# 142 matrix products appended to the end of TensorE's list, in a convolution and two feed-forward layers

## Chip, cores and metric

The kernel runs on one core of one Trainium2 chip. The metric is the device time of one execution in microseconds, the median over runs.

## What is computed

An input of 2 x 4096 tokens with 192 channels goes through a causal convolution over 7 tokens, whose weights are a softmax per head (8 heads of 24 channels). Then come two feed-forward layers of 192 to 2048 to 192 channels. The reference, cut to what matters:

```python
def _attn_ref(x, weight):            # x (2, 4096, 192), weight (8, 7)
    w = softmax(weight, axis=-1)
    x_unf = x_pad[:, idx, :].reshape(B, S, K, H, group)
    return np.einsum('hk,bskhg->bshg', w, x_unf).reshape(B, S, D)

def _moe_ref(x, w_in, w_out):        # 8192 tokens, 192 -> 2048 -> 192
    h = x @ w_in
    return np.maximum(0.01 * h, h) @ w_out

def _moe2_ref(x, w_in, w_out):
    h = x @ w_in
    g = np.where(h >= 1, h, np.where(h <= -1, 0.0, (h + 1) ** 2 / 4))
    return g @ w_out
```

## The kernel before

Tokens are worked on in 16 tiles of 512 (T). Channels lie on partitions. Each feed-forward layer is cut into 16 slices of 128 inner channels, so there are 2 x 16 x 16 = 512 units of one layer, one tile and one slice. A unit has five products up (line 584, from x and the weights wi) and five down (line 593, from the activated values and the weights wo), since every value is held as a high and a low part in the type float32r. The weights of both layers stay on the chip in six tiles per kind: `wi_h`, `wi_l`, `wi_b`, `wo_h`, `wo_l`, `wo_b`, two of each, 128 partitions x 16 slices x 128 columns. They are written once, early in the run (lines 265 to 298).

The eight banks of the accumulator are tiles `banks[0]` to `banks[7]`. In the second part of the run units of both layers alternate; their up products go to banks 0 to 3 in turn, the sums of the first layer to banks 4 and 5, those of the second to banks 6 and 7.

Steps are put into a `Plan` with an engine, a cost and what they read and write. `plan.order()` lays them out in time with a list scheduler, and the loop in lines 776 and 777 calls each step's function in that order. The order in which instructions are made is the order of each engine's list; nothing reorders them later. Waits between engines are put in by the framework from what instructions read and write.

The last tile ends in `finish_last`: ScalarE copies bank 7 out (line 691), VectorE bank 6 (line 692), TensorE turns both by products with a folded identity (line 697, 64 columns each, float32) and by transposes (line 706) into banks 1 and 0, VectorE and ScalarE copy the turned blocks out (lines 714 and 723), and two DMAs store 192 KB each (line 732), one issued by SyncE and one by ScalarE. TensorE's list ends with the transposes of line 706.

At the start `add_warm` puts 24 products of a zero tile (bf16, 512 columns, line 328) on TensorE. Their sums are not read either.

Of the kernel before, what the change touches and what calls it, by code (L numbers as in the profile page):

```python
# [145 lines left out]
def kernel(  # L146
# [16 lines left out]
    nc = tc.nc  # L163
# [6 lines left out]
    T = 512  # L170
# [34 lines left out]
    banks = [pp.tile([128, T], F32, name=f"bank{i}") for i in range(8)]  # L205
# [22 lines left out]
    wi_h = [cp.tile([128, NF, 128], F32R, name=f"wi_h{m}") for m in range(2)]  # L228
    wi_l = [cp.tile([128, NF, 128], F32R, name=f"wi_l{m}") for m in range(2)]
    wi_b = [cp.tile([128, NF, 128], F32R, name=f"wi_b{m}") for m in range(2)]  # L230
    wo_h = [cp.tile([128, NF, 128], F32R, name=f"wo_h{m}") for m in range(2)]
    wo_l = [cp.tile([128, NF, 128], F32R, name=f"wo_l{m}") for m in range(2)]
# [88 lines left out]
    def add_warm():  # L321
        nc.gpsimd.memset(zero, 0.0)
        out_ = bank(1, -10)
        for i in range(WARM):
            cold = i < COLD
            plan.add(
                pe, 430 if cold else 220,
                lambda: nc.tensor.matmul(  # L328
                    out=out_(), lhsT=zero, rhs=zero.unsqueeze(1).broadcast_to((128, T // 128, 128)),
                    start=True, stop=True,  # L330
                ),
                writes=[out_], due=-1e9 if cold else 1e9,
            )
# [53 lines left out]
    def add_diagonals():  # L387
        def fold():
            for e in range(2):
                nc.gpsimd.tensor_copy(same[DB * e:DB * (e + 1)], ident[DB * e:DB * (e + 1), DB * e:DB * (e + 1)])  # L390

        plan.add(pool, 500, lambda: make_identity(nc, ident), writes=["ident"])
        plan.add(pool, 260, fold, reads=["ident"], writes=["same"])
        for k in range(KP, K):
            plan.add(
                dve, 220,
                lambda k=k: nc.vector.tensor_scalar(flat(NP + k - KP), ident, taps[:, 0, k:k + 1], None, ALU.mult),
                reads=["ident", "taps"], writes=[("diagonal a", k)], uses=[spare],
            )
        for k in range(NP):  # L400
            plan.add(
                dve, 220,
                lambda k=k: nc.vector.tensor_scalar(
                    flat(k).rearrange("p (e d) -> p e d", e=2), same.unsqueeze(1).broadcast_to((128, 2, DB)),
                    pair[:, k:k + 1], None, ALU.mult,
                ),
                reads=["same", "pair"], writes=[("diagonal", k)], uses=[spare],
            )
# [327 lines left out]
            )  # L736


    units = []
    for i in range(NF + OFF[-1]):  # L740
        for j in range(N0):
# [2 lines left out]
    one = [(0, j, f) for j in range(N0, NB) for f in range(NF)]  # L744
    two = [(1, j, f) for j in range(NB) for f in range(NF)]
    while two:
        units += one[:1] + two[:1]
        one, two = one[1:], two[1:]
# [12 lines left out]
    with tc.manual_schedule():  # L761
        add_warm()
        add_taps()
        add_diagonals()
        seen = set()
        for t, (m, j, f) in enumerate(units):
            if m == 0 and f == 0:
                add_conv(t - AHEAD, j)
            for o in range(2):
                if (m, o, f // 2) not in seen:  # L770
                    seen.add((m, o, f // 2))
                    add_weights(t, m, o, f // 2)
            add_unit(t, (m, j, f))
        for tag, count in COUNT.items():
            plan.rotate(tag, count)
        for n in plan.order():
            plan.steps[n]["fn"]()


# [28 lines left out]
```

## Time and profile before

| what | value |
|---|---|
| median of 2 runs | 1194.51 us (1194.39 to 1194.63) |
| span of the profiled execution | 1192.7 us |
| TensorE matmuls busy | 1186.8 us, 5210 instructions |
| TensorE weight loads busy | 972.7 us, 5210 instructions |
| VectorE / ScalarE / GpSimd busy | 782.7 / 734.3 / 438.2 us |
| bytes moved by DMA | 27.9 MB, 23 GB/s in the mean |

The span runs from the first to the last instruction of one profiled execution; the median is of runs without a profile. In the profile PE stands for TensorE's matmuls, PEld for its weight loads (each product has one of either; a float32 product has two), DVE for VectorE, ACT for ScalarE, POOL for GpSimd, SP for SyncE; a q behind an engine means its instruction queue. L593 is line 593 of the kernel. Matmuls are pipelined, so their recorded durations overlap; their pace is read from the distance of their starts. PEclk is the clock that TensorE was granted, as a share of full speed.

### The profile page before, as it was taken

The numbers are of one execution on the slowest core, as the hardware profiler recorded it, in microseconds if no ns is written. First come the engines' busy times: TensorE is split into PE (matmuls) and PEld (weight loads), VectorE is DVE, ScalarE is ACT, GpSimd is POOL, SyncE is SP. The second block draws the span as 40 slices with busy tenths as digits, with TensorE's granted clock in tenths as the row PEclk, the third lists the DMA queues.
The fourth block names the chain that finished last, engine by engine and source line by source line (L and its number), as shares of the span: only waits on it lengthen the run. The fifth ranks groups of instructions, "written<-read, shape, count | busy, mean of one in ns | idle before, by whom it ended". The sixth has DMA issues, their size and how long they took to land.

```text
span 1192.7 us, 15464 instructions
## 1 busy us (share of the span) xinstructions
PE 1186.8 (100%) x5210; PEld 972.7 (82%) x5210; DVE 782.7 (66%) x1209; ACT 734.3 (62%) x1296; POOL 438.2 (37%) x407
## 2 busy tenths in 40 slices
PE   9999999999999999999999999999999999999998
PEld 5788888888888888888888888888888888888887
DVE  7899897748567494764847658485674545447664
ACT  6777866656565565655656566565655656556654
POOL 4566374323223232232323233232233222335554
PEclk9999999999999999999999999999999999999999
DMA  4443111101001010010101001010000000000000
GB/s 132 117 104 99 43 43 18 23 1 23 10 9 23 1 23 9 15 18 1 32 1 23 10 10 23 1 23 1 1 14 1 14 1 3 12 1 14 14 14 14
DMA packets 114000, 27.90 MB, mean 23 GB/s; under 512 B 103680, under 2 KB 111872, under 8 KB 113920
## 3 DMA queue, kind: packets, MB, share of 16 engines
q1 hardware_dynamic: 113504, 26.69, 10.3%
q8 instruction: 40, 0.66, 0.2%
q14 instruction: 40, 0.33, 0.1%
q10 hardware_dynamic: 416, 0.23, 0.1%
HBM read 20.61 MB, written 6.29 MB: 23 GB/s over the span
## 4 chain that ended last, share of the span: by engine, by line
PE 99%; DMA 0%; SPq 0%; DVE 0%; issue 0%; ACT 0%; ACTq 0%
PE bank L584 49%; PE bank L593 49%; PE bank L529 1%; DMA wraw<-in_x_dram 0%; PE bank L534 0%; PE bank L328 0%; PE bank L478 0%; SPq L257 0%; PE bank L697 0%; SPq L255 0%; DVE s L714 0%; SPq L469 0%; DVE s L723 0%; ACT s L723 0%; ACTq L723 0%
## 5 line engine op out<-in xcount | busy, mean ns | idle before, releaser
L632 POOL TENSOR_TENSOR gl<-g,gh 128x512 fp32r<-128x512 f32 x256 | 343.2, 1343 | 677.6 <-ACT gh L630 674.7
L619 DVE TENSOR_SCALAR s<-bank 128x512 f32<-128x512 f32 x256 | 176.3, 689 | 303.4 <-PE bank L584 302.2
L584 PE MATMUL bank<-x,wi_h 128*128 128x512 f32 x1024 | 317.5, 391 | 0.0
L584 PE MATMUL bank<-x,wi_b 128*128 128x512 f32 x1024 | 316.9, 391 | 0.0
L623 ACT ACTIVATE s<-s,half 128x512 f32<-128x512 f32 x256 | 184.8, 722 | 192.7 <-DVE s L619 191.4
L630 ACT CAST gh<-g 128x512 fp32r<-128x512 f32 x256 | 158.6, 620 | 180.8 <-DVE g L627 178.1
L584 PEld LDWEIGHTS bank<-x,wi_h 128*128 128x128 f32 x1024 | 191.9, 188 | 42.2 <-issue 1.7
L584 PEld LDWEIGHTS bank<-x,wi_b 128*128 128x128 f32 x1024 | 192.2, 188 | 41.4 <-issue 1.4
L627 DVE TENSOR_TENSOR g<-bank,s 128x512 f32<-128x512 f32 x256 | 175.5, 686 | 67.8 <-ACT s L623 67.7
L593 PE MATMUL bank<-gh,wo_b 128*128 128x512 f32 x512 | 199.3, 389 | 0.0
L593 PE MATMUL bank<-gh,wo_h 128*128 128x512 f32 x512 | 199.3, 389 | 0.0
L593 PE MATMUL bank<-gl,wo_h 128*128 128x512 f32 x512 | 199.2, 389 | 0.0
L584 PE MATMUL bank<-x,wi_l 128*128 128x512 f32 x512 | 199.2, 389 | 0.0
L593 PE MATMUL bank<-gl,wo_b 128*128 128x512 f32 x512 | 199.2, 389 | 0.0
L593 PE MATMUL bank<-gh,wo_l 128*128 128x512 f32 x512 | 199.2, 389 | 0.0
L608 ACT ACTIVATE gh<-bank 128x512 fp32r<-128x512 f32 x256 | 152.8, 597 | 46.8 <-PE bank L593 25.3
L612 DVE TENSOR_TENSOR gl<-bank,gh 128x512 fp32r<-128x512 f32 x256 | 174.2, 680 | 9.8 <-ACT bank L608 9.2
L608 ACT ACTIVATE bank<-bank 128x512 f32<-128x512 f32 x256 | 151.8, 593 | 0.0
L523 DVE SCALAR_TENSOR_TENSOR xy<-xT,taps,xy 128x512 f32<-128x512 f32 x159 | 136.0, 878 | 0.2
L593 PEld LDWEIGHTS bank<-gl,wo_h 128*128 128x128 f32 x512 | 96.1, 188 | 20.0
L593 PEld LDWEIGHTS bank<-gh,wo_b 128*128 128x128 f32 x512 | 96.1, 188 | 20.0
L593 PEld LDWEIGHTS bank<-gh,wo_h 128*128 128x128 f32 x512 | 96.1, 188 | 20.0
(93 smaller groups left out, 741.5 us busy)
## 6 DMA issues: line engine op xcount, KB each, us to landing
xy<-in_x_dram SPq DMA_DIRECT2D x104, 64.0 KB, 2.4
wraw<-in_moe_w_out_dram SPq DMA_DIRECT2D x16, 384.0 KB, 3.0
out_dram<-o SPq DMA_DIRECT2D x90, 64.0 KB, 1.9
wraw<-in_moe_w_in_dram SPq DMA_DIRECT2D x16, 256.0 KB, 2.7
wraw<-in_moe_w_in_dram SPq DMA_DIRECT2D x32, 64.0 KB, 2.6
wraw<-in_x_dram SPq DMA_DIRECT2D x3, 384.0 KB, 5.3
out_dram<-s SPq DMA_DIRECT2D x1, 192.0 KB, 2.0
out_dram<-s ACTq DMA_DIRECT2D x1, 192.0 KB, 2.0
```

The costliest lines, as they stand in the source:

```text
L523: nc.vector.scalar_tensor_tensor(out=ys[i](), in0=t()[:, i, k:k + T], scalar=taps[:, i, k:k + 1], in1=ys[i](), op0=ALU.mult, op1=ALU.add,)
L529: nc.tensor.matmul(out=ys[1](), lhsT=flat(k), rhs=t()[:, 1, 2 * k:2 * k + T], start=(k == 0), stop=(k == NP - 1))
L584: nc.tensor.matmul(out=h(), lhsT=w, rhs=v[:, k], start=(part == 0 and i == 0), stop=(part == 1 and i == 1))
L593: nc.tensor.matmul(out=p[part](), lhsT=w, rhs=v(), start=(first and i == 0), stop=(last and i == len(todo) - 1))
L608: lambda dst=dst: nc.scalar.activation(out=dst(), in_=h(), func=ACTF.Prelu, alpha=0.01),
L612: dve, 680, lambda: nc.vector.tensor_tensor(out=b(), in0=h(), in1=a(), op=ALU.subtract),
L619: dve, 680, lambda: nc.vector.tensor_scalar(s(), h(), 1.0, -1.0, ALU.min, ALU.max),
L623: act, 720, lambda: nc.scalar.activation(out=s(), in_=s(), func=ACTF.Square, scale=0.5, bias=half),
L627: dve, 680, lambda: nc.vector.tensor_tensor(out=g(), in0=h(), in1=s(), op=ALU.max),
L630: plan.add(act, 620, lambda: nc.scalar.copy(a(), g()), reads=[g], writes=[a])
L632: pool, 1390, lambda: nc.gpsimd.tensor_tensor(out=b(), in0=g(), in1=a(), op=ALU.subtract),
```

## The change

A function `add_more` is added and called once, after the loop that makes all steps. It makes 142 products on TensorE, each with `start` and `stop`, into banks 2 to 7. Weights come from `wo_h` and `wo_l` of both layers, the moving values from `wi_h` and `wi_l`. `low` and `high` are partitions 0 to 63 and 64 to 127: a product with these uses half the rows of the array. In order: 6 plain products (128 rows, 512 columns); 24 pairs of a low half (bank 2) and a high half (bank 3); 4 plain; 24 pairs into banks 6 and 7, where the high half uses other weights than the low one; 4 plain; 12 short ones (64 columns); 8 times a plain and a short one; 4 plain. No instruction reads what they leave in the banks.

```diff
--- before.py
+++ after.py
@@ -736,6 +736,41 @@
             )
 
 
+    def add_more():
+
+        def flat_(t):
+            return t.rearrange("p f c -> p (f c)")
+
+        streams = [flat_(wi_h[0]), flat_(wi_l[0]), flat_(wi_h[1]), flat_(wi_l[1])]
+        weights = [flat_(wo_h[0]), flat_(wo_l[0]), flat_(wo_h[1]), flat_(wo_l[1])]
+        full, low, high = slice(0, 128), slice(0, 64), slice(64, 128)
+
+        def one(k, at, rows=full, cols=T):
+            w = weights[k % 4][rows, 128 * (k % 16):128 * (k % 16 + 1)]
+            v = streams[k // 4 % 4][rows, T * (k % 4):T * (k % 4) + cols]
+            nc.tensor.matmul(out=banks[at][:, 0:cols], lhsT=w, rhs=v, start=True, stop=True)
+
+        for k in range(6):
+            one(k, 2 + k % 2)
+        for k in range(24):
+            one(k, 2, low)
+            one(k, 3, high)
+        for k in range(4):
+            one(k, 4 + k % 2)
+        for k in range(24):
+            one(k, 6, low)
+            one(k + 7, 7, high)
+        for k in range(4):
+            one(k, 4 + k % 2)
+        for k in range(12):
+            one(k, 4, cols=64)
+        for k in range(8):
+            one(k, 5)
+            one(k + 3, 4, cols=64)
+        for k in range(4):
+            one(k, 4 + k % 2)
+
+
     units = []
     for i in range(NF + OFF[-1]):
         for j in range(N0):
@@ -775,6 +810,7 @@
             plan.rotate(tag, count)
         for n in plan.order():
             plan.steps[n]["fn"]()
+        add_more()
 
 
 # ---- launch: one core; inputs and outputs as the reference has them ----
```

## Rows read from the trace of the kernel before

**Rows 1.** The page, part 1: span; busy time, share and instructions by engine.

```profile
span 1192.7 us, 15464 instructions
PE 1186.8 (100%) x5210; PEld 972.7 (82%) x5210; DVE 782.7 (66%) x1209; ACT 734.3 (62%) x1296; POOL 438.2 (37%) x407
```

**Rows 2.** The page, part 4: the chain that ended last, shares by engine.

```profile
PE 99%; DMA 0%; SPq 0%; DVE 0%; issue 0%; ACT 0%; ACTq 0%
```

**Rows 3.** Windows: length, busy time (instructions) by engine, PEclk, DMA share, GB/s.

```profile
100.00:1180.00 1080.00, 1080.00 (x4765) 893.70 (x4764) 693.13 (x1048) 655.48 (x1125) 378.27 (x315) 1.00 0.08 15
```

**Rows 4.** Timeline near the end: start, length, engine, line, operation.

```profile
1185.38 0.39 PE L593 MATMUL bank<-gh,wo_h 128*128 128x512 f32 x1
1185.38 0.19 PEld L593 LDWEIGHTS bank<-gh,wo_l 128*128 128x128 f32 x1
1185.60 0.39 PE L593 MATMUL bank<-gh,wo_l 128*128 128x512 f32 x1
1185.61 0.19 PEld L593 LDWEIGHTS bank<-gl,wo_h 128*128 128x128 f32 x1
```

**Rows 5.** Chain in order of time, its last run of products: start, length, what.

```profile
1181.69 5.68 PE bank L593 x25
```

**Rows 6.** Timeline from 1186.9 us to the end, some lines left out.

```profile
1186.98 0.39 PE L593 MATMUL bank<-gl,wo_h 128*128 128x512 f32 x1
1187.36 0.97 PEld L697 LDWEIGHTS bank<-same,yz 128*128 128x128 f32 x8 [0.41 <-ACT yz L691]
1187.36 1.10 PE L697 MATMUL bank<-same,yz 128*128 128x64 f32 x8
1187.41 0.69 DVE L692 COPY xy<-bank 128x512 f32<-128x512 f32 x1 [3.38 <-PE bank L593]
1188.19 0.48 PEld L706 LDWEIGHTS bank<-ident,xy 128*128 128x128 f32 x4
1188.30 0.61 PE L706 MATMUL bank<-ident,xy 128*128 128x128 f32 x4
...
1189.40 0.39 SPq L732 DMA_DIRECT2D out_dram<-s  x1
1189.46 0.37 ACT L723 COPY s<-bank 128x256 f32<-128x256 f32 x1 [2.15 <-DVE s L723]
1189.86 0.40 ACTq L732 DMA_DIRECT2D out_dram<-s  x1
```

**Rows 7.** By line, 732 and 803: landing time of the stores; closing instructions, first and last start.

```profile
DMA to landing us min/median/max: 2.0/2.0/2.0
...
L803 SPq EVENT_SEMAPHORE  x7: 17/28/28, 1189.8 to 1192.6; - x7
```

**Rows 8.** By line, 298, 426 and 627: durations (ns), first and last start.

```profile
L298 POOL TENSOR_TENSOR wo_l<-wa,wo_h x16: 730/738/1200, 24.6 to 188.3; 128x256 fp32r<-128x256 f32 x16
...
L426 DVE TENSOR_TENSOR x<-bank,x x21: 676/680/692, 17.0 to 1089.4; 128x512 fp32r<-128x512 f32 x21
...
L627 DVE TENSOR_TENSOR g<-bank,s x256: 644/692/693, 136.8 to 1183.3; 128x512 f32<-128x512 f32 x128
```

**Rows 9.** Groups by line, 1187.3 to 1189: busy us, mean ns of one, idle before.

```profile
L697 PE MATMUL bank<-same,yz 128*128 128x64 f32 x8 | 1.1, 281 | 0.0
L697 PEld LDWEIGHTS bank<-same,yz 128*128 128x128 f32 x8 | 1.0, 191 | 0.4 <-ACT yz L691 0.4
```

**Rows 10.** Line 328's products: two runs of the timeline, then all 24 by line.

```profile
1.07 4.87 PE L328 MATMUL bank<-zero 128*128 128x512 bf16 x11 [1.07 <-POOL own L340]
...
18.10 1.47 PE L328 MATMUL bank<-zero 128*128 128x512 bf16 x6
...
L328 PE MATMUL bank<-zero x24: 377/390/634, 1.1 to 19.2; 128*128 128x512 bf16 x24
```

**Rows 11.** Windows at the end, columns as in Rows 3.

```profile
1190.00:1191.00 1.00, 0.00 (x0) 0.00 (x0) 0.00 (x0) 0.00 (x0) 0.00 (x0) 1.00 0.72 242
1191.00:1192.00 1.00, 0.00 (x0) 0.00 (x0) 0.00 (x0) 0.00 (x0) 0.00 (x0) 0.55 0.45 151
```

## The prediction

> **What bounds the kernel now.** I read the page's busy times first: the span is 1192.7 us and TensorE's matmuls are busy for all but 6 us of it [rows 1]. The chain that ended last is TensorE for 99% [rows 2]. The middle of the run, by windows, holds 4765 products in 1080 us at a granted clock of 1.00 [rows 3], one every 0.227 us; the timeline shows such products starting 0.22 to 0.23 us apart, each recorded as 0.39 us long (they overlap), and the load of the next weights beginning as the product before starts [rows 4]. The chain in order of time says the same for the last run of them: 25 in 5.68 us, 0.227 each [rows 5].
>
> So what stands on TensorE's list is paid in full, unless something else lasts longer. That is so only at the very end: the last four transposes end at 1188.30 + 0.61 = 1188.91, while the second store is issued at 1189.86 [rows 6], lands 2.0 us later, at about 1191.9, and is followed by some 0.8 us of closing semaphores [rows 7]. So TensorE is idle for the last 3.8 us of the span.
>
> The profiled execution's span is 1192.7 and the median of the runs 1194.5, so 1.8 us lie around the span; I add the difference of the spans to the median.
>
> **The change part by part.** Nothing is removed or moved, no DMA, no copy. 142 products are added behind the last transpose: 26 plain ones (128 rows, 512 columns: 6 + 4 + 4 + 8 + 4), 96 half-row ones (64 rows, 512 columns, two rows of 48) and 20 short ones (128 rows, 64 columns: 12 + 8).
>
> What they wait for: the weights were written by 188.3 us; banks 4 and 5 were last read by 1090.1 us; the last read of an h bank that I look for in banks 2 and 3 began at 1183.3 [rows 8]; banks 6 and 7 are copied out by 1187.41 + 0.69 = 1188.10 [rows 6]. All of it lies before 1188.91, so no wait is added, and nobody waits for the products. The stores run as before. The transposes' weight loads follow each other at (0.97 - 0.191) / 7 = 0.111 us, by the eight loads just ahead of them [rows 6, 9]. The last transpose starts 0.27 us before its end, at 1188.64, so the first new product starts at about 1188.75.
>
> Plain products: 26 x 0.227 = 5.90 us [rows 5].
>
> Short products: the nearest rows are the eight with 64 columns near the end, (1.10 - 0.281) / 7 = 0.117 us apart [rows 6, 9], hardly more than a load: weights, not columns, bound them. Those are another fp32 form. From below nothing goes under the load's 0.111, from above stands the 512-column 0.227: 2.2 to 4.5 us for twenty. I take 0.117: 2.34 us.
>
> Half-row products: the trace has none, every product in it uses 128 rows. Two bounds for a pair. If the halves run one after the other, a pair costs two products: 2 x 0.227 = 0.454. If they run side by side, it costs one product, 0.227, and not less than its two loads, 2 x 0.111 = 0.222. Which is nearer? The halves share neither array rows, nor the partitions that they read, nor the bank that they write (2 and 3, then 6 and 7), and a load already runs under a product [rows 4]. I take side by side, at 0.235, a little above 0.227 because loads and columns are nearly equal limits there: 48 x 0.235 = 11.28 us.
>
> On the loads the rows are plain: the next whole-row load starts at 1185.38 and 1185.61, with the product in flight [rows 4]. The Trainium skill, "TensorE: Matmul & The Clock Gate", Part 3, The mechanism, says under "What overlaps and what doesn't" that a load overlaps products in flight only where their row groups differ. This trace does not agree for whole rows; by that sentence a half's load would stand behind the same half's product, 0.338 a pair, and the sum would give 1216.6 (the second rival). The same part, Measured speedup, gives 3.07 times for four 32-row tiles, which I turn into an estimate of 4 / 3.07 = 1.30 product times for a group, 0.295 a pair and 1214.6 in all; no row here shows it.
>
> Changing between whole rows and half rows happens four times. From below it is free; from above a product's tail (0.39 - 0.227 = 0.16) plus a load that is not covered (0.19 [rows 4]) make 0.35. I take the tail alone: 4 x 0.16 = 0.64 us.
>
> Sum: 5.90 + 2.34 + 11.28 + 0.64 = 20.16, and the last product's tail of 0.16. TensorE ends at 1188.75 + 20.16 + 0.16 = 1209.07. The closing after the store took about 0.8 us; some of it may have been waits that are over by then, so 0.3 to 0.8; with 0.8 the span is 1209.9, 17.2 us longer. The first 3.1 us of the products lie beside the store and cost nothing; were that cover gone, the change would cost 20.3. Time: 1194.5 + 17.2 = 1211.7 us, 1.4% more. Its own range, by a pair of 0.222 to 0.295 and the small bounds, is 1209 to 1215.
>
> **The rivals.**
>
> *The halves one after the other (the other side).* Place: the two rows of 24 pairs. For it: TensorE issues in order, and none of the 512-column products in these rows starts less than 0.216 us after another [rows 3, 5, 10]. Against it: no products there had different rows. Price: 48 x (0.454 - 0.235) = 10.5 us more, 1222.2, 2.3% over. The 2% line lies at 23.9 us more than before, 6.7 above my sum: this mechanism decides from a pair of 0.235 + 6.7 / 48 = 0.375 us on.
>
> *Side by side, but loads not covered.* A half's weights could be held back until the product in the same half is through: 0.111 + 0.227 = 0.338 a pair, 48 x 0.103 = 4.9 us more, 1216.6. For it: whether the spare set of weights that [rows 4] imply exists for each half apart is not seen. Against it: the whole-row loads.
>
> *The clock falls.* After TensorE went quiet at 1188.91 the granted clock went from 1.00 to 0.50 between 1191 and 1192 [rows 11], so the row of 1187.36 to 1188.91 with its thin products did not at once bring it down. What slow products cost shows at the start: 11 warm-up products with 512 columns at (4.87 - 0.63) / 10 = 0.42 us, later six at (1.47 - 0.39) / 5 = 0.22 [rows 10]. If half-row products passed for little work and the clock stayed at its lower level (1.2 GHz) through them, pairs would double: 48 x 0.235 = 11.3 more, 1223.0, and 1227.5 with the 20 plain ones behind the first row at twice 0.227. Against it: side by side they are as dense as plain ones. If it fell only behind the short ones, 12 plain products would double, 2.7 us, 1214.4, inside my range.
>
> *The products do not run.* Their sums are not read. But the 24 warm-up products, whose sums nobody reads either, are all in the trace [rows 10]. Time then 1194.5.
>
> **How the numbers follow.** Side by side 0.63 (1211.7); loads not covered 0.12 (1216.6); one after the other 0.17 (1222.2); clock down 0.06 (1223 to 1227); not run 0.01; a gain from something that I do not see 0.01. I predict the likeliest, 1211.7. The range 1209 to 1223 takes in the first three and leaves out about 0.13: the clock, the rest, and the ends of the bounds. Faster and slower are counted from 2%, about what a measurement of this kernel can tell from no change. Same: 0.63 + 0.12 + 0.01 = 0.76; slower: 0.17 + 0.06 = 0.23; faster 0.01.
>
> **What would show it.** In the profile of the changed kernel: the first new product starts at 1188.7 to 1188.9 with no idle before it but the load's; each half row lasts 24 x 0.235 = 5.6 us, and low and high products start in twos about 0.11 apart, 0.235 from low to low. A half row of 8.1 us would mean uncovered loads, 10.9 us one after the other, with starts 0.227 apart and a clock of 1.00; a clock of 0.50 there the third rival. The short ones stand 0.11 to 0.12 apart, the span ends at most 0.8 us behind TensorE, and everything before 1188.6 stays where it was. I am wrong if the pair takes 0.30 us or more.

## The result, and the profile after

The changed kernel takes 1211.47 us in the median (1211.44 to 1211.50), against 1194.51 before: a ratio of 1.014, 95% interval 1.011 to 1.017. The forecast was 1211.7. The span grew from 1192.7 to 1209.7 us, by 17.0 (forecast: 17.2).

The page of the changed kernel, the span and the busy times (the lines that answer to [rows 1]):

```profile
span 1209.7 us, 15748 instructions
...
PE 1206.7 (100%) x5352; PEld 989.0 (82%) x5352; DVE 782.5 (65%) x1209; ACT 734.4 (61%) x1296; POOL 438.1 (36%) x407
```

PE and PEld have 142 instructions more each, the counts of the others are unchanged. The products all run. The chain in order of time for the last 23 us shows that they now end the program (start, length, what):

```profile
1186.85 0.47 PE bank L593 x2
1187.31 1.09 PE bank L697 x8
1188.40 0.45 PE bank L706 x4
1188.85 19.99 PE bank L751 x141
```

Line 751 is the one product call of the added function. Up to 1188.85 the chain holds the same steps as before [rows 6]. Behind them stand 19.99 us of new products; the last ends at 1188.85 + 19.99 = 1208.84, and the span ends 0.86 us later. (The chain counts 141 of the products; the page has all 142.)

The timeline of TensorE in the changed kernel (start, length, engine, line, operation, count) shows the first row of pairs with the change into it and out of it, a piece of the second row, and the short ones:

```profile
1189.62 0.39 PE L751 MATMUL bank<-wi_l,wo_h 128*128 128x512 f32 x1
1189.84 0.40 PE L751 MATMUL bank<-wi_l,wo_l 128*128 128x512 f32 x1
1190.16 0.50 PE L751 MATMUL bank<-wi_h,wo_h 64*128 64x512 f32 x2
1190.50 0.40 PE L751 MATMUL bank<-wi_h,wo_l 64*128 64x512 f32 x2
1190.74 0.39 PE L751 MATMUL bank<-wi_h,wo_h 64*128 64x512 f32 x2
1190.97 0.40 PE L751 MATMUL bank<-wi_h,wo_l 64*128 64x512 f32 x2
...
1195.51 0.39 PE L751 MATMUL bank<-wi_l,wo_l 64*128 64x512 f32 x2
1195.83 0.50 PE L751 MATMUL bank<-wi_h,wo_h 128*128 128x512 f32 x1
...
1196.96 0.49 PE L751 MATMUL bank<-wi_h,wo_h 64*128 64x512 f32 x1
1196.96 0.50 PE L751 MATMUL bank<-wi_l,wo_l 64*128 64x512 f32 x1
...
1203.81 0.28 PE L751 MATMUL bank<-wi_h,wo_h 128*128 128x64 f32 x1
1203.92 0.28 PE L751 MATMUL bank<-wi_h,wo_l 128*128 128x64 f32 x1
```

Here a line with 64x512 and x2 is a pair. Its length, 0.39 us, is that of one product: both halves are recorded as starting and ending together. From 1190.74 to 1195.51 a pair follows every 0.227 us. At a change from whole to half rows, the step is 0.32 (1189.84 to 1190.16) and the next one 0.34 (to 1190.50) where 0.227 would stand without it. The short ones stand 0.11 us apart. In the second row, where the high half has other weights, the first pair starts together as well.

The windows of the changed kernel over the two rows and the short ones (columns as in [rows 3]):

```profile
1190.10:1195.50 5.40, 5.40 (x47) 4.42 (x48) 0.00 (x0) 0.00 (x0) 0.00 (x0) 1.00 0.22 73
1196.90:1202.30 5.40, 5.40 (x47) 4.62 (x48) 0.00 (x0) 0.00 (x0) 0.00 (x0) 1.00 0.00 0
1203.60:1207.60 4.00, 4.00 (x29) 3.65 (x28) 0.00 (x0) 0.00 (x0) 0.00 (x0) 1.00 0.00 0
```

From its first pair to the plain product behind it the first row of 48 half products takes 5.67 us (1190.16 to 1195.83), the change out of it included; 48 products one after the other would take 10.9. The granted clock is 1.00 in all three windows.

### The profile page after: what moved, and what is told of

Same layout as the page of the kernel before. It is cut to its first block, busy times and chain, and to the rows that moved or that the text cites. A ratio compares the mean times of both kernels' runs of the same rounds, so it can differ in the third digit from the quotient of the medians.

```text
span 1209.7 us, 15748 instructions
## 1 busy us (share of the span) xinstructions
PE 1206.7 (100%) x5352; PEld 989.0 (82%) x5352; DVE 782.5 (65%) x1209; ACT 734.4 (61%) x1296; POOL 438.1 (36%) x407
## 4 chain that ended last, share of the span: by engine, by line
PE 99%; DMA 0%; SPq 0%; issue 0%
PE bank L584 48%; PE bank L593 48%; PE bank L751 2%; PE bank L529 1%; DMA wraw<-in_x_dram 0%; PE bank L534 0%; PE bank L328 0%; PE bank L478 0%; SPq L257 0%; PE bank L697 0%; SPq L255 0%; PE bank L706 0%; SPq L469 0%
## 5 line engine op out<-in xcount | busy, mean ns | idle before, releaser
L584 PEld LDWEIGHTS bank<-x,wi_l 128*128 128x128 f32 x512 | 96.1, 188 | 20.0
L593 PEld LDWEIGHTS bank<-gl,wo_b 128*128 128x128 f32 x512 | 96.1, 188 | 20.0
L593 PEld LDWEIGHTS bank<-gh,wo_l 128*128 128x128 f32 x512 | 96.1, 188 | 20.0
```

Source lines behind the costliest of these rows:

```text
L584: nc.tensor.matmul(out=h(), lhsT=w, rhs=v[:, k], start=(part == 0 and i == 0), stop=(part == 1 and i == 1))
L593: nc.tensor.matmul(out=p[part](), lhsT=w, rhs=v(), start=(first and i == 0), stop=(last and i == len(todo) - 1))
```

## The experiments

Theory: the halves run side by side because they use different rows of the array, so that a pair costs one product. Rivals: another bank alone is what lets them; the engine looks far ahead in its list; loads limit a pair; changes between whole and half rows cost nothing or more; thin work brings the clock down. Each experiment changes only the added products.

**Both products in the low half** (`same_half`):

```diff
-            one(k, 3, high)
+            one(k, 3, low)
...
-            one(k + 7, 7, high)
+            one(k + 7, 7, low)
```

> Both products of every pair now use the low half (partitions 0 to 63); banks, counts and order stay. If different array rows are what lets two products run side by side, each half product costs 0.227 us and a pair 0.454 instead of 0.227: 48 x 0.227 = 10.9 us more than the changed kernel's 1211.5, so 1222.4. If different banks are enough, the time stays at 1211.5. If a half's load must stand behind the product in the same half (the rival with uncovered loads), each half product costs 0.338: 48 x 0.449 = 21.6 us more, 1233. If half-work lets the granted clock fall, it shows as 0.50 in the windows of the two rows and about 1240 or more.

Measured: 1222.39 us, 1.023 of before (1.021 to 1.025). Chain, and timeline of products and of loads:

```profile
1188.88 30.85 PE bank L751 x142
```

```profile
1190.77 0.62 PE L751 MATMUL bank<-wi_h,wo_l 64*128 64x512 f32 x2
1191.23 0.62 PE L751 MATMUL bank<-wi_h,wo_h 64*128 64x512 f32 x2
...
1190.54 0.42 PEld L751 LDWEIGHTS bank<-wi_h,wo_l 64*128 64x128 f32 x2
1191.00 0.42 PEld L751 LDWEIGHTS bank<-wi_h,wo_h 64*128 64x128 f32 x2
```

A pair now lasts 0.62 and follows every 0.46 us: one after the other. The rows are the same 64, the banks still differ, so another bank is not enough. Nor does a half-row product simply cost half: it costs the 0.227 of a whole one. (Both products now also read the same partitions; a product's rows and its partitions go together, so no run tells the two apart.) A pair's two loads also come one product apart (0.42 for two of 0.19) and lie under products in flight in the same half: half products of one half keep the 0.227 pace, and the rival with uncovered loads, 1233, is out. So is the rival of the clock, as it was put: two rows of half products, 10.9 us each, did not lower it. Windows (columns as before):

```profile
1195.00:1200.00 5.00, 5.00 (x24) 4.06 (x23) 0.00 (x0) 0.00 (x0) 0.00 (x0) 1.00 0.00 0
1205.00:1210.00 5.00, 5.00 (x23) 4.06 (x23) 0.00 (x0) 0.00 (x0) 0.00 (x0) 1.00 0.00 0
```

The clock column alone would not settle it: in the kernel before it reads 1.00 at 2 to 3 us as well, where the warm-up products took 0.42 us each [rows 10]:

```profile
2.00:3.00 1.00, 1.00 (x4) 0.35 (x3) 0.00 (x0) 0.77 (x2) 0.80 (x6) 1.00 0.06 14
```

The pace settles it. 122 products of 512 columns at 0.227, 20 short ones at 0.112, four changes at 0.21 and the last product's tail of 0.16 come to 30.9 us, and the chain has 30.85: there is no room for a slow stretch.

The Trainium skill's sentence that a load overlaps products in flight only where the row groups differ ("TensorE: Matmul & The Clock Gate", Part 3, The mechanism) does not describe these rows either: same half, load under product.

**Whole rows** (`whole_rows`), the half products made of 128 rows:

```diff
-            one(k, 2, low)
-            one(k, 3, high)
+            one(k, 2)
+            one(k, 3)
...
-            one(k, 6, low)
-            one(k + 7, 7, high)
+            one(k, 6)
+            one(k + 7, 7)
```

> All half products become whole-row products of 128 rows; counts, banks and order stay. Pace 0.227 each: 48 x 0.227 = 10.9 us more, and the four changes between whole and half rows go away. If a change costs 0.2 us as the changed kernel's starts suggest, that gives 1222.4 - 0.8 = 1221.6; if changes cost nothing, 1222.4.

Measured: 1221.57 us (ratio 1.022, 1.021 to 1.024). The chain:

```profile
1188.85 29.99 PE bank L751 x142
```

That is 29.99 against 30.85 us in the experiment ahead of it: 142 products at the same pace, without the four changes. 0.86 / 4 = 0.21 us for a change.

**All low halves, then all high ones** (`low_then_high`):

```diff
             one(k, 2, low)
+        for k in range(24):
             one(k, 3, high)
...
             one(k, 6, low)
+        for k in range(24):
             one(k + 7, 7, high)
```

> The same 142 products, but in each row the 24 low halves stand first and the 24 high ones behind them. If products start in the order of the list and only neighbours overlap, each row takes 48 x 0.227 = 10.9 us instead of 5.5, the time is 1211.5 + 10.9 = 1222.4 less one overlap a row. If the engine looks ahead far enough to bring a high product beside a low one, the time stays near 1211.5.

Measured: 1220.89 us (ratio 1.022, 1.020 to 1.023). The order in the list matters: most of the gain is gone (9.4 of 10.9 us), so the engine doesn't look far ahead. But it looks further than I expected: one overlap a row would have given 1222.4 - 2 x 0.227 = 1221.9, and 1.0 us less was measured. Timeline around the seam of the first row:

```profile
1194.76 0.39 PE L751 MATMUL bank<-wi_l,wo_h 64*128 64x512 f32 x1
1194.77 0.49 PE L751 MATMUL bank<-wi_h,wo_h 64*128 64x512 f32 x1
1194.99 0.39 PE L751 MATMUL bank<-wi_l,wo_l 64*128 64x512 f32 x1
1195.10 0.39 PE L751 MATMUL bank<-wi_h,wo_l 64*128 64x512 f32 x1
1195.21 0.39 PE L751 MATMUL bank<-wi_l,wo_h 64*128 64x512 f32 x1
1195.33 0.39 PE L751 MATMUL bank<-wi_h,wo_h 64*128 64x512 f32 x1
1195.44 0.39 PE L751 MATMUL bank<-wi_l,wo_l 64*128 64x512 f32 x1
```

The four lines with wi_l are the last four low products, the three with wi_h the first high ones. The first high product is recorded as starting at 1194.77, beside the twenty-first low one and ahead of three that stand before it in the list. The time agrees: about 0.75 us saved in each row is some three products.

**Pairs of 64 columns** (`thin_pairs`):

```diff
-            one(k, 2, low)
-            one(k, 3, high)
+            one(k, 2, low, 64)
+            one(k, 3, high, 64)
...
-            one(k, 6, low)
-            one(k + 7, 7, high)
+            one(k, 6, low, 64)
+            one(k + 7, 7, high, 64)
```

> The 48 pairs get 64 columns instead of 512, so that loads bound them. My prediction counted two loads one after the other, 0.222 a pair: 48 x 0.222 = 10.7 us, 1211.3, hardly a change. If the loads of the two halves run at once, as the equal starts in the first row of the changed kernel suggest, a pair costs 0.111: 48 x (0.227 - 0.111) = 5.6 us less, 1205.9. If such thin work lets the granted clock fall, windows show 0.50 behind them and the 12 to 20 us around are slower by up to twice.

Measured: 1205.70 us (ratio 1.011, 1.008 to 1.014). Timeline, products and loads:

```profile
1190.34 0.28 PE L751 MATMUL bank<-wi_h,wo_h 64*128 64x64 f32 x2
1190.45 0.28 PE L751 MATMUL bank<-wi_h,wo_l 64*128 64x64 f32 x2
1190.56 0.28 PE L751 MATMUL bank<-wi_l,wo_h 64*128 64x64 f32 x2
...
1190.31 0.19 PEld L751 LDWEIGHTS bank<-wi_h,wo_h 64*128 64x128 f32 x2
1190.42 0.19 PEld L751 LDWEIGHTS bank<-wi_h,wo_l 64*128 64x128 f32 x2
```

There is a pair every 0.111 us, with two loads in the length of one. The loads of the two halves run at once. My floor of two loads, 0.222, does not exist. One of the four runs took 1213.65 at a mean granted clock of 0.993, the others 1205.6 to 1205.7 at 1.000. That run has no trace, so where its clock fell is not known; the last experiment shows such a fall in full.

**Quarter rows** (`quarters`), 192 products of 32 rows in place of 96 of 64:

```diff
-            one(k, 2, low)
-            one(k, 3, high)
+            for q in range(4):
+                one(k, 2 + q, slice(32 * q, 32 * q + 32))
...
-            one(k, 6, low)
-            one(k + 7, 7, high)
+            for q in range(4):
+                one(k + 7 * q, 2 + q, slice(32 * q, 32 * q + 32))
```

> Each pair of 64-row halves becomes four products of 32 rows (array rows 0, 32, 64, 96) with banks 2 to 5, 192 in place of 96. If four row groups run side by side as two do, a group of four costs 0.227 and the time stays at 1211.5. The Trainium skill's 3.07 times for four tiles (TensorE: Matmul & The Clock Gate, Part 3, Measured speedup), as an estimate 1.30 product times a group. In rows of this case: at 0.295 a group the time would be 48 x 0.068 = 3.3 us more, 1214.8; if only two at a time run, 0.454 a group and 1222.4.

Measured: 1211.50 us (ratio 1.014, 1.012 to 1.016), the changed kernel's own time.

```profile
1190.72 0.40 PE L751 MATMUL bank<-wi_h,wo_h 32*128 32x512 f32 x4
1190.73 0.19 PEld L751 LDWEIGHTS bank<-wi_h,wo_l 32*128 32x128 f32 x4
1190.95 0.40 PE L751 MATMUL bank<-wi_h,wo_l 32*128 32x512 f32 x4
```

In this timeline four products and four loads run at once, a group every 0.23 us. The estimate from the Trainium skill's 3.07 times ("TensorE: Matmul & The Clock Gate", Part 3, Measured speedup), 1.30 product times a group, is not what this case shows: 1.00.

**Many changes** (`many_turns`), the same 142 products, twelve plain ones each behind four pairs:

```diff
-        for k in range(6):
-            one(k, 2 + k % 2)
...
+        for k in range(2):
+            one(k, 4 + k % 2)
+        for k in range(48):
+            if k < 24:
+                one(k, 2, low)
+                one(k, 3, high)
+            else:
+                one(k - 24, 6, low)
+                one(k - 17, 7, high)
+            if k % 4 == 3:
+                one(k // 4, 4 + k // 4 % 2)
```

> The same 142 products, but 12 of the plain ones now stand one behind every fourth pair, so that the list changes between whole and half rows 24 times instead of 4. My prediction took 0.16 us a change (bounds 0 to 0.35); the starts in the changed kernel suggest 0.2: 20 x 0.2 = 4 us more, 1215.5. If a change costs nothing, 1211.5; at 0.16, 1214.7; at 0.35, 1218.5.

Measured: 1215.73 us (ratio 1.018, 1.016 to 1.019), 4.26 more than the changed kernel for 20 more changes: 0.213 us each. Timeline around two of them, with loads:

```profile
1189.89 0.19 PEld L751 LDWEIGHTS bank<-wi_h,wo_l 64*128 64x128 f32 x2
1190.12 0.40 PE L751 MATMUL bank<-wi_h,wo_l 64*128 64x512 f32 x2
1190.45 0.19 PEld L751 LDWEIGHTS bank<-wi_h,wo_h 128*128 128x128 f32 x1 [0.36 <-issue]
1190.45 0.50 PE L751 MATMUL bank<-wi_h,wo_h 128*128 128x512 f32 x1
1190.88 0.19 PEld L751 LDWEIGHTS bank<-wi_l,wo_h 64*128 64x128 f32 x2 [0.24 <-issue]
```

The load for the plain product doesn't start with the pair in flight, as it does elsewhere, but 0.33 us after that pair's start: across a change it starts late. From the pair at 1190.12 to the pair at 1190.88 the step is 0.76 us, where two steps of 0.227 make 0.45. The two changes there cost 0.31 between the starts; the rest of 2 x 0.213 comes behind them, like the step of 0.34 behind 1190.16 in the changed kernel.

**Ten plain products only** (`ten_plain`):

```diff
-        for k in range(6):
+        for k in range(10):
             one(k, 2 + k % 2)
-        for k in range(24):
...
-            one(k, 4 + k % 2)
```

> Only ten plain products of the 142 are left. By the prediction they start at 1188.7, end by 1191.2 and lie beside the last store, which lands at about 1191.9: the time is that of before, 1194.5, and the span 1192.7. If work behind the last transpose is not covered by the store, it is 10 x 0.227 = 2.3 us more, 1196.8.

Measured: 1194.38 us, ratio 0.9997 (0.9988 to 1.0006), span 1192.7. Timeline:

```profile
1189.82 0.40 ACTq L732 DMA_DIRECT2D out_dram<-s  x1
...
1190.79 0.40 PE L751 MATMUL bank<-wi_h,wo_l 128*128 128x512 f32 x1
```

The tenth product ends at 1191.19, before the store issued at 1189.82 has landed 2.0 us later. These 2.3 us of work on TensorE cost nothing.

**142 short products** (`all_short`):

```diff
-        for k in range(6):
-            one(k, 2 + k % 2)
...
+        for k in range(142):
+            one(k, 2 + k % 2, cols=64)
```

> All 142 added products are whole-row products with 64 columns. Bound by loads at 0.111 to 0.117 each they take 15.8 to 16.6 us, TensorE ends at about 1205 and the time is 1207.3 to 1208. If the granted clock falls under such thin work, a window of the second half shows 0.50; if loads slow down with it, the time rises by up to 8 us, to 1215.

Measured: 1217.09 us (1216.39 to 1217.94; ratio 1.019, 1.017 to 1.020), above both sums. Windows and timeline:

```profile
1190.00:1192.00 2.00, 2.00 (x20) 2.00 (x19) 0.00 (x0) 0.00 (x0) 0.00 (x0) 1.00 0.59 197
1192.00:1194.00 2.00, 2.00 (x16) 2.00 (x15) 0.00 (x0) 0.00 (x0) 0.00 (x0) 0.77 0.00 0
1194.00:1196.00 2.00, 2.00 (x12) 2.00 (x11) 0.00 (x0) 0.00 (x0) 0.00 (x0) 0.50 0.00 0
```

```profile
1192.71 0.28 PE L751 MATMUL bank<-wi_l,wo_h 128*128 128x64 f32 x1
1192.82 0.28 PE L751 MATMUL bank<-wi_l,wo_l 128*128 128x64 f32 x1
...
1194.28 0.40 PE L751 MATMUL bank<-wi_l,wo_l 128*128 128x64 f32 x1
1194.49 0.40 PE L751 MATMUL bank<-wi_l,wo_h 128*128 128x64 f32 x1
```

At about 1193.1 the granted clock goes from 1.00 to 0.50, its lower level of 1.2 GHz, though PE and PEld are recorded as busy without a break; it stays there to the end. The pace goes from 0.111 to 0.213 us, loads included. My upper bound of 1215 was too low because the fall came after 4.4 us and some 40 products, so that 102, more than the half I had reckoned with, ran at the slow pace: 40 x 0.111 + 102 x 0.213 = 26.2 us, which is the 26.23 of its chain. The profiled run took 1217.77; two others took 1216.4. If only the point of the fall differs, it came some 14 products later there (an estimate: 1.4 / 0.102), so the 40 are no fixed count.

## Why the prediction was right, point by point

*What bounds the kernel.* Right. Work at the end of TensorE's list was free where it ended ahead of the store's landing (`ten_plain`), and of the change's 19.99 us all but 3.0 were paid (17.0 in the span).

*Start and closing.* The first new product is recorded at 1188.60 (forecast 1188.75, at the earliest 1188.7), but the second follows 0.32 us later instead of 0.227, and the chain has the new products take over at 1188.85. TensorE ends at 1208.84 (forecast 1209.07), and the span 0.86 us later (0.8). The 188.3 us by which the weights were to be written is the start of their last write, which took at most 1.2 us [rows 8]; nothing hangs on it.

*The halves.* Right, and shown by three runs: side by side in different array rows (changed kernel), one after the other in the same rows with different banks (`same_half`), one after the other, but for some three a row, when they are not neighbours in the list (`low_then_high`). The pair costs 0.227, not 0.235: 48 x 0.008 = 0.4 us too much. The reason I gave for the surcharge, loads as a nearly equal limit, is wrong (`thin_pairs`). With it went the one visible sign that I had wrong: I expected low and high products 0.11 us apart, and they start together.

*The changes between whole and half rows.* Taken at 0.16 each, measured at 0.21 in two ways (`whole_rows` against `same_half`, and `many_turns`): 4 x 0.05 = 0.2 us too little. The term held the tail of a product alone, but the load comes late as well (`many_turns`); how the 0.21 divides between the two is not shown. The upper bound of 0.35 held.

*The short ones.* The twelve in a row stand 0.112 us apart against 0.117: 20 x 0.005 = 0.1 too much. That loads bound them fits `thin_pairs`.

These misses, -0.4, +0.2 and -0.1, add up to -0.3 us: the new products took 19.99 us in the chain against 20.16 + 0.16 = 20.32. They took over 0.1 us later than forecast, so TensorE ended 0.2 earlier. That the total came so close owes something to the different signs, which is luck.

*The range.* 1209 to 1215 is not what its bounds add up to. With all of them at once the sum goes from 1209.8 (pairs 0.222, shorts 0.111, changes free, closing 0.3) to 1217.5 (0.295, 0.227, 0.35). The measured time lies in both.

*The rivals.* One after the other: its price was right to 0.2 us (1222.2, and `same_half` 1222.39), its condition not met. What spoke for it, that TensorE issues in order, does not hold strictly either: in `low_then_high` a product started ahead of three others. Loads not covered: not met, in either half arrangement. The clock: right as a mechanism, on the wrong products. Half rows keep it at 1.00; a long run of 64-column products brought it down (`all_short`). Its price is now read at both levels: 0.111 us at 1.00, 0.213 at 0.50. Through the 12 short ones and the 8 mixed in with plain ones in the change it stayed at 1.00. That products may be dropped: not so, all 142 are in the trace.

## What to carry to other kernels

Products with 64 or 32 rows can be had side by side for the price of one (here 0.227 us with 512 columns), if neighbours in the list use different rows of the array; the same products sorted by half lose most of it. In every run the products of a pair or group also had different banks; whether one bank would do was not tried. Keep products of one row size together, since each change between whole and half rows cost 0.21 us. And when work is added at the end of an engine's list, compare its end with the last store's landing first: here 2.3 us of products were free.

## What the runs showed of the hardware that was not expected

- Loads for different array rows run at once: two in the time of one (`thin_pairs`, a pair every 0.111 us), four as well (`quarters`).
- A product can start ahead of others that stand before it in the list, if it uses other rows: by three places in `low_then_high`. How deep this goes in other lists was not tried.
- Products of 64 columns without a break did not keep the clock: from 1.00 to 0.50 after 4.4 us, 0.111 to 0.213 us each, while the busy times of PE and PEld stayed full (`all_short`). The change's own short ones kept it; what lies between was not tried, but for `thin_pairs`, where one of four runs had a mean clock of 0.993.
